# GpSimd takes the q and k products (from VectorE) and the residual adds (from DMA) in a fused linear-attention and gated-FFN kernel

## The chip, the cores and the metric

The kernel runs on one core of a Trainium2 chip. The metric is the device time of one execution in microseconds (us); less is better. Times are medians of several executions. A profiled execution gives the busy time of each engine, the waits and the exact order of the instructions. In the profile PE is TensorE's matmuls, PEld its weight loads, DVE is VectorE, ACT is ScalarE, POOL is GpSimd and SP is SyncE.

## The reference

A complex-decay linear attention feeds a gated feed-forward network, with the attention's result `x` added at the end.

```python
# q, k, v, a_re, a_im: (4, 8, 768, 48) float32
mag = sqrt(a_re**2 + a_im**2); scale = minimum(mag, 0.999) / (mag + 1e-6)
ar_n, ai_n = a_re * scale, a_im * scale
for t in range(768):                       # per batch and head, state 48 x 48
    S_re, S_im = ar*S_re - ai*S_im + k_t v_t^T,  ar*S_im + ai*S_re
    y_t = q_t @ S_re
x = y as (3072, 384)
g, val = x @ w_gate, x @ w_val             # 384 x 1536
res_gate = sigmoid(x @ w_res)              # 384 x 384
out = x + res_gate * ((gelu(g) * val) @ w_out)
```

The kernel does not walk the time steps. It takes 256 of them at once (a group `g`, two 128-row chunks). It builds the cumulated log decay and angle with matmuls against triangular matrices, takes `E = exp(+)`, `Ei = exp(-)` and the cosines and sines `CS`, and forms `Q = CS*(q*E)` and `K = CS*(k*Ei)`. Masked products of these give the attention within a group, and a small state is carried between groups.

## The kernel before

There are 12 groups in 7 units (1, 2, 2, 2, 2, 2 and 1 groups). The program alternates `phase_x(u)`, a *decay stretch*, and `phase_y(u)`, a *gate/value stretch*. In the decay stretch of unit `u` ScalarE makes the exponentials and sines of the next unit, and TensorE ends the attention of unit `u` and does the output matmuls of unit `u-1`. In the gate/value stretch TensorE runs the gate and value matmuls of unit `u`, while VectorE multiplies `q`, `k` by the decay for unit `u+1`. `weave` interleaves steps at issue; each engine then runs its own list strictly in order.

```python
ldv = pool("ldv", bufs=6); pK = pool("pK", bufs=1); xp = pool("xp", bufs=10); ob = pool("ob", bufs=2)
# (pool construction is shortened here)

def load_v(g):
    t = ldv.tile([128, C, H, D], BF, tag="v", name="v")
    for c in range(C):
        nc.gpsimd.dma_start(out=t[:, c], in_=rows(v, g, c))     # GpSimd's queue
    T["v", g] = t

def after_landing(t, f):                    # f's transfers start only once t has landed
    w = singles.tile([1, 1], FP, name="landed%d" % len(T))
    i = nc.gpsimd.tensor_copy(out=w, in_=t[0:1, C - 1, H - 1, D - 1:D])
    with tc.issue_after(i.ins):
        f()

def turn(nm, g, srcs):                      # decay rows, turned by way of DRAM
    md = dr.tile([n, DM], FP, tag="d" + nm, name="d" + nm)
    for i, src in enumerate(srcs):
        nc.gpsimd.dma_start(out=md[i:i + 1, :], in_=src)
    m = mp.tile([128, n, H], FP, tag=nm, name=nm)
    for u in range(2):
        nc.gpsimd.dma_start(out=m[u * D:(u + 1) * D].rearrange("p r h -> p (r h)"), in_=...)
    # ...

def products(g):
    def x0():
        qE = pK.tile([128, W], BF, tag="qE", name="qE")
        nc.vector.tensor_tensor(out=qE, in0=flat(T["q", g]), in1=T["E", g], op=OP.mult)
        T["qE", g] = qE
    def x1():
        kE = pK.tile([128, W], BF, tag="kE", name="kE")
        nc.vector.tensor_tensor(out=kE, in0=flat(T["k", g]), in1=T["Ei", g], op=OP.mult)
        T["kE", g] = kE
    def mk(nm, src):
        def x():                            # Q = CS*qE, K = CS*kE
            # ...
            nc.vector.tensor_tensor(out=t, in0=T["CS", g], in1=sb, op=OP.mult)
        return x
    return [x0, mk("Q", "qE"), x1, mk("K", "kE")]

def gv_step(u, ffi):
    # ... three matmuls into PSUM tile gp, three into vp
    act(out=h2[:, ffi, :], in_=gp, func=AF.Gelu)
    nc.vector.scalar_tensor_tensor(out=h2[:, ffi, :], in0=h2[:, ffi, :], scalar=0.5, in1=vp, ...)

def op_step(u, jj):
    # ... 12 matmuls into PSUM tile ps
    ot = ob.tile([128, DM], FP, tag="ot", name="ot")
    nc.vector.scalar_tensor_tensor(out=ot, in0=T["sg", u][:, jj], scalar=1.0, in1=ps, op0=OP.add, op1=OP.mult)
    t0 = token(u, jj) * 128
    if u == NU - 1:
        nc.vector.tensor_tensor(out=ot, in0=ot, in1=T["x", token(u, jj)], op=OP.add)
    nc.sync.dma_start(out=out[t0:t0 + 128, :], in_=ot)
    if u < NU - 1:                          # residual added by an accumulating DMA
        nc.gpsimd.dma_start(out=out[t0:t0 + 128, :], in_=T["x", token(u, jj)], accum_op=OP.add)

def phase_y(u):
    # ...
    pr = [st for g in gs(u + 1) for st in products(g)]
    weave((0.0, 1.0, gv), (0.0, 0.4, pr), (0.3, 0.95, att_steps(u + 1, 0)))

for u in range(-1, NU + 1):
    phase_x(u)
    # ... decay inputs of later units
    phase_y(u)
    for g in gs(u + 3):
        load_q(g)                           # q and k, on SyncE's queue
        after_landing(T["k", g], call(load_v, g))
```

## Time and profile before

| | before |
|---|---|
| time, median of 3 (range) | 324.13 us (323.16 to 324.32) |
| span of the profiled execution | 322.4 us |
| TensorE / VectorE / ScalarE / GpSimd busy | 84% / 73% / 65% / 25% |

The first part of the page gives each engine's busy time, share of the span and number of instructions.

```profile
PE 272.1 (84%) x2200; PEld 170.5 (53%) x2200; DVE 234.8 (73%) x431; ACT 209.8 (65%) x353; POOL 80.5 (25%) x115
```

A mean hides that the stretches have different limits, so the next view cuts the span. The table of windows has start and end, length, the busy time of each engine (instructions in brackets), the granted TensorE clock, the share of time that the 16 DMA engines were busy (summed so that it can pass 1) and the rate. I cut where ScalarE loads a new function table, which is where stretches begin. The rows are the gate/value stretch of unit 0, the decay stretch of unit 1 and the gate/value stretch of unit 1.

```profile
core 0: us, PE busy (x) PEld busy (x) DVE busy (x) ACT busy (x) POOL busy (x), PEclk, DMA share, GB/s
63.20:83.50 20.30, 19.24 (x224) 15.63 (x224) 16.25 (x36) 12.16 (x27) 3.87 (x6) 0.83 1.20 171
83.50:101.40 17.90, 14.09 (x81) 7.48 (x80) 13.59 (x24) 17.19 (x28) 3.93 (x6) 1.00 1.34 190
101.40:127.80 26.40, 25.30 (x269) 16.01 (x267) 23.53 (x42) 16.57 (x31) 8.37 (x12) 1.00 0.96 153
...
```

In gate/value stretches TensorE is nearly always busy (25.30 of 26.40 us); in decay stretches ScalarE is (17.19 of 17.90).

The groups of instructions (line, engine, operation, output and inputs, shapes, count, then busy us, mean ns, idle before it) give the price of the products on VectorE.

```profile
L309 DVE TENSOR_TENSOR qE<-q,E 128x768 bf16<-128x768 f32 x12 | 11.4, 950 | 6.8 <-DMA ar<-in_a_re_dram 3.5 <-ACT E L124 3.3
L321 DVE TENSOR_TENSOR Q<-CS,qE 128x1536 bf16<-128x1536 bf16 x12 | 11.4, 947 | 2.5 <-ACT CS L124 2.5
L314 DVE TENSOR_TENSOR kE<-k,Ei 128x768 bf16<-128x768 f32 x12 | 11.4, 946 | 0.0
```

The timeline of GpSimd between 50 and 86 us (start us, length us, instruction, and in brackets how long the engine waited and for what) shows the two small copies that hold back `v` until `k` has landed.

```profile
...
69.91 0.17 POOL L171 COPY landed<-k 1x1 f32<-1x1 f32 x1 [19.59 <-DMA k<-in_k_dram]
70.14 1.77 POOL L150 DMA_DIRECT2D v<-in_v_dram  x2
74.41 0.17 POOL L171 COPY landed<-k 1x1 f32<-1x1 f32 x1 [2.50 <-DMA k<-in_k_dram]
74.64 1.76 POOL L150 DMA_DIRECT2D v<-in_v_dram  x2
```

GpSimd has nothing else to do in that time, so a wait of 19.59 us costs nothing.

Finally the timeline of VectorE around the start of unit 1's gate/value stretch at 101.4 us.

```profile
100.11 0.94 DVE L321 TENSOR_TENSOR Q<-CS,qE 128x1536 bf16<-128x1536 bf16 x1
100.98 0.94 DVE L314 TENSOR_TENSOR kE<-k,Ei 128x768 bf16<-128x768 f32 x1
101.84 0.94 DVE L309 TENSOR_TENSOR qE<-q,E 128x768 bf16<-128x768 f32 x1
102.71 0.94 DVE L321 TENSOR_TENSOR K<-CS,kE 128x1536 bf16<-128x1536 bf16 x1
103.58 1.27 DVE L446 SCALAR_TENSOR_TENSOR h<-h,vp 128x512 bf16<-128x512 bf16 x2
```

The products run one after another at 0.94 us.

### The profile page before, as it was taken

The numbers are of one execution on the slowest core, as the hardware profiler recorded it, in microseconds if no ns is written. First come the engines' busy times: TensorE is split into PE (matmuls) and PEld (weight loads), VectorE is DVE, ScalarE is ACT, GpSimd is POOL, SyncE is SP. The second block draws the span as 40 slices with busy tenths as digits, with TensorE's granted clock in tenths as the row PEclk, the third lists the DMA queues.
The fourth block names the chain that finished last, engine by engine and source line by source line (L and its number), as shares of the span: only waits on it lengthen the run. The fifth ranks groups of instructions, "written<-read, shape, count | busy, mean of one in ns | idle before, by whom it ended". The sixth has DMA issues, their size and how long they took to land.

```text
span 322.4 us, 5853 instructions
## 1 busy us (share of the span) xinstructions
PE 272.1 (84%) x2200; PEld 170.5 (53%) x2200; DVE 234.8 (73%) x431; ACT 209.8 (65%) x353; POOL 80.5 (25%) x115
## 2 busy tenths in 40 slices
PE   0337927789887999789997999998999999899994
PEld 0116624677543666445664556554656655555682
DVE  2446769968499995599982999974899837864352
ACT  4549684646998557977568976569665683656150
POOL 1206522022040370259020572000630003200220
PEclk9995676959999999999999999999999999999998
DMA  8999999989999995396850595000360003600441
GB/s 159 218 183 181 182 169 165 185 174 180 187 179 186 223 160 33 76 197 113 122 36 2 107 121 95 2 0 3 75 122 3 2 0 76 122 2 0 107 91 50
DMA packets 137755, 34.55 MB, mean 107 GB/s; under 512 B 126848, under 2 KB 137728, under 8 KB 137728
## 3 DMA queue, kind: packets, MB, share of 16 engines
q1 hardware_dynamic: 103296, 23.60, 36.8%
q0 software_dynamic: 34432, 10.59, 31.2%
q8 instruction: 17, 0.28, 0.3%
q14 instruction: 10, 0.08, 0.1%
HBM read 31.31 MB, written 9.07 MB: 125 GB/s over the span
## 4 chain that ended last, share of the span: by engine, by line
PE 56%; SPq 12%; ACT 11%; DMA 9%; DVE 6%; issue 3%; POOL 1%; ACTq 0%; DVEq 0%; POOLq 0%
PE vp L443 14%; PE gp L439 13%; SPq L136 6%; SPq L144 6%; PE op L463 6%; DMA k<-in_k_dram 4%; PE rp L455 3%; PE tp L349 3%; PE tp L346 3%; PE at L356 3%; ACT L477 3%; DMA m<-dm 3%; ACT s L124 3%; PE cst L236 2%; PE y L394 2%
## 5 line engine op out<-in xcount | busy, mean ns | idle before, releaser
L124 ACT ACTIVATE h<-gp 128x512 bf16<-128x512 f32 (+1 forms) x84 | 44.5, 536 | 38.4 <-PE gp L439 37.9
L439 PE MATMUL gp<-xT,wg 128*128 128x512 bf16 (+1 forms) x252 | 65.4, 353 | 3.4 <-ACT h L124 2.0
L443 PE MATMUL vp<-xT,wv 128*128 128x512 bf16 (+1 forms) x252 | 66.6, 353 | 0.0
L446 DVE SCALAR_TENSOR_TENSOR h<-h,vp 128x512 bf16<-128x512 bf16 (+1 forms) x84 | 49.8, 603 | 16.4 <-PE vp L443 12.0
L463 PE MATMUL op<-wo,h 128*128 128x384 bf16 x288 | 50.2, 326 | 8.1 <-ACT Ei L124 5.9
L463 PEld LDWEIGHTS <-h 128*128 128x128 bf16 x288 | 27.8, 98 | 28.7 <-issue 11.3
L351 ACT COPY qk<-tp 96x512 bf16<-96x512 bf16 x48 | 27.9, 580 | 17.1 <-PE tp L349 7.9
L359 DVE TENSOR_TENSOR atm<-at,mask 128x512 bf16<-128x512 f32 x48 | 32.9, 686 | 8.2 <-PE at L356 7.8
L472 POOL DMA_DIRECT2D out_dram<-x x22 | 20.4, 947 | 54.4 <-DMA out_dram<-ot 43.1
L439 PEld LDWEIGHTS <-wg 128*128 128x128 bf16 x252 | 23.7, 99 | 17.9 <-issue 4.2
L443 PEld LDWEIGHTS <-wv 128*128 128x128 bf16 x252 | 23.8, 99 | 13.3
L189 DVE TENSOR_TENSOR ai<-s,ai 128x768 f32<-128x768 f32 x12 | 11.1, 955 | 23.6 <-ACT s L124 23.6
L477 ACT ACT_TABLE_LOAD x21 | 26.9, 1283 | 1.1 <-PEq L615 0.7
L346 PE MATMUL tp<-ident,Q 128*96 128x128 bf16 x192 | 20.1, 231 | 6.9 <-DVE Q L321 6.2
L346 PEld LDWEIGHTS <-Q 128*96 128x96 bf16 x192 | 17.4, 130 | 15.3 <-DVE Q L321 10.0
L124 ACT ACTIVATE CS<-fg,hpi 128x768 bf16<-128x768 f32 x12 | 11.2, 935 | 20.8 <-DVE fg L246 20.7
L150 POOL DMA_DIRECT2D v<-in_v_dram x24 | 21.9, 932 | 4.2 <-DMA v<-in_v_dram 1.3
L349 PE MATMUL tp<-ident,K 128*96 128x128 bf16 x192 | 22.3, 235 | 0.0
L236 PE MATMUL cst<-ai,lt0b 128*128 128x384 f32 x24 | 11.8, 577 | 11.7 <-ACT ai L124 11.0
L352 DVE COPY qk<-tp 96x512 bf16<-96x512 bf16 x48 | 19.8, 413 | 2.3 <-ACT qk L351 1.7
L212 PE MATMUL csl<-ar,lt0a 128*128 128x384 f32 x24 | 11.4, 562 | 10.8 <-DMA ar<-in_a_re_dram 10.8
L466 DVE SCALAR_TENSOR_TENSOR ot<-sg,op 128x384 f32<-128x384 f32 x24 | 13.1, 547 | 10.1 <-PE op L463 10.1
(85 smaller groups left out, 522.0 us busy)
## 6 DMA issues: line engine op xcount, KB each, us to landing
ar<-in_a_re_dram SPq DMA_DIRECT2D x24, 192.0 KB, 4.7
ai<-in_a_im_dram SPq DMA_DIRECT2D x24, 192.0 KB, 4.1
q<-in_q_dram SPq DMA_DIRECT2D x24, 192.0 KB, 3.8
k<-in_k_dram SPq DMA_DIRECT2D x24, 192.0 KB, 3.7
out_dram<-ot SPq DMA_DIRECT2D x24, 192.0 KB, 2.5
out_dram<-x POOLq DMA_DIRECT2D x22, 192.0 KB, 3.7
v<-in_v_dram POOLq DMA_DIRECT2D x24, 96.0 KB, 5.0
wg<-in_moe_w_gate_dram POOLq DMA_DIRECT2D x4, 288.0 KB, 11.4
```

The lines of the kernel that those rows point to most:

```text
L124: tab(nc.scalar.activation(**kw))
L150: nc.gpsimd.dma_start(out=t[:, c], in_=rows(v, g, c))
L346: nc.tensor.transpose(out=tp[0:DD, j * 128:j * 128 + 128], in_=Q(x), identity=ident)
L349: nc.tensor.transpose(out=tp[0:DD, 512 + j * 128:640 + j * 128], in_=K(x), identity=ident)
L351: nc.scalar.copy(out=qk[0:DD, 0:512], in_=tp[0:DD, 0:512])
L359: nc.vector.tensor_tensor(out=atm, in0=at, in1=mask4, op=OP.mult)
L439: nc.tensor.matmul(out=gp, lhsT=wg[:, fi, ffi * 128:(ffi + 1) * 128], rhs=xT[:, fi, :], start=(fi == 0), stop=(fi == KD - 1))
L443: nc.tensor.matmul(out=vp, lhsT=wv[:, fi, ffi * 128:(ffi + 1) * 128], rhs=xT[:, fi, :], start=(fi == 0), stop=(fi == KD - 1))
L446: nc.vector.scalar_tensor_tensor(out=h2[:, ffi, :], in0=h2[:, ffi, :], scalar=0.5, in1=vp, op0=OP.mult, op1=OP.mult)
L463: nc.tensor.matmul(out=ps, lhsT=h2[:, ffi, jj * 128:(jj + 1) * 128], rhs=wo[:, ffi, :], start=(ffi == 0), stop=(ffi == KF - 1))
L472: nc.gpsimd.dma_start(out=out[t0:t0 + 128, :], in_=T["x", token(u, jj)], accum_op=OP.add)
L477: tab(nc.scalar.preload_act_table_set(nm))
```

## The change

VectorE looks loaded (73%) and GpSimd free (25%). The change gives GpSimd the 24 products `q*E` and `k*Ei`, those of `q` only after the sines, with a second buffer each (`v` and `x` lose one of theirs). GpSimd also adds `x` into the output tile, so that one store is enough and the 22 accumulating DMAs go. The decay rows move to SyncE's queue, to leave GpSimd free. `v` loads lose the wait for `k` in later units and are issued ahead of the gate/value stretch; only the loads issued at `u = -1` keep it. The four steps of a group are issued as qE, kE, Q, K.

```diff
-    ldv = ctx.enter_context(tc.tile_pool(name="ldv", bufs=6))
+    ldv = ctx.enter_context(tc.tile_pool(name="ldv", bufs=5))
-    pK = ctx.enter_context(tc.tile_pool(name="pK", bufs=1))
+    pK = ctx.enter_context(tc.tile_pool(name="pK", bufs=2))
-    xp = ctx.enter_context(tc.tile_pool(name="xp", bufs=10))
+    xp = ctx.enter_context(tc.tile_pool(name="xp", bufs=9))
@@ p2_sin
+        T["sin"] = T["tab"]
@@ turn: both DMA issues
-            nc.gpsimd.dma_start(...)
+            nc.sync.dma_start(...)
@@ products
-            nc.vector.tensor_tensor(out=qE, in0=flat(T["q", g]), in1=T["E", g], op=OP.mult)
+            i = nc.gpsimd.tensor_tensor(out=qE, in0=flat(T["q", g]), in1=T["E", g], op=OP.mult)
+            tc.add_manual_dep(i.ins, T["sin"].ins.name, behind, reason="after the sines")
-            nc.vector.tensor_tensor(out=kE, in0=flat(T["k", g]), in1=T["Ei", g], op=OP.mult)
+            nc.gpsimd.tensor_tensor(out=kE, in0=flat(T["k", g]), in1=T["Ei", g], op=OP.mult)
@@ op_step
-        if u == NU - 1:
-            nc.vector.tensor_tensor(out=ot, in0=ot, in1=T["x", token(u, jj)], op=OP.add)
+        eng = nc.vector if u == NU - 1 else nc.gpsimd
+        eng.tensor_tensor(out=ot, in0=ot, in1=T["x", token(u, jj)], op=OP.add)
         nc.sync.dma_start(out=out[t0:t0 + 128, :], in_=ot)
-        if u < NU - 1:
-            nc.gpsimd.dma_start(out=out[t0:t0 + 128, :], in_=T["x", token(u, jj)], accum_op=OP.add)
@@ phase_y
-        pr = [st for g in gs(u + 1) for st in products(g)]
+        pr = [pp[i] for pp in [products(g) for g in gs(u + 1)] for i in (0, 2, 1, 3)]
@@ main loop
+        if u > 0:
+            for g in gs(u + 2):
+                load_v(g)
         phase_y(u)
         for g in gs(u + 3):
             load_q(g)
-            after_landing(T["k", g], call(load_v, g))
+            if u < 0:
+                after_landing(T["k", g], call(load_v, g))
```

More of the change, by code (lines that the diff above doesn't have):

```diff
@@ L115 @@
     order = mybir.DependencyInfo(mybir.DependencyClass.NoSync, mybir.DependencyReason.DATA)
+    behind = mybir.DependencyInfo(mybir.DependencyClass.Sync, mybir.DependencyReason.DATA)
     def tab(ins):
@@ L261, in turn @@
         for i, src in enumerate(srcs):
-            nc.gpsimd.dma_start(out=md[i:i + 1, :], in_=src)
+            nc.sync.dma_start(out=md[i:i + 1, :], in_=src)
         m = mp.tile([128, n, H], FP, tag=nm, name=nm)
         for u in range(2):
-            nc.gpsimd.dma_start(out=m[u * D:(u + 1) * D].rearrange("p r h -> p (r h)"),
+            nc.sync.dma_start(out=m[u * D:(u + 1) * D].rearrange("p r h -> p (r h)"),
                                 in_=md.rearrange("r (h d) -> d (r h)", h=H))
```

## The prediction

> **What bounds it now.** The table of windows gives three regimes. (a) 0–58 us: loads and a serial ScalarE/VectorE chain; TensorE is busy 29 of 58 us. (b) Later, long gate/value stretches with TensorE saturated (25.9 of 26.0, 26.4 of 26.4, 26.3 of 26.3 us). (c) Between them, 14–20 us decay stretches in which ScalarE leads (17.1 of 19.2 us) and TensorE idles 1–4 us each, about 12 us in all. VectorE is 73% busy, but only in (c) does it hold anything: the timeline shows the sines waiting 1.16 + 0.83 us (and 0.93 + 1.16) for the fractions.
>
> **What the change does.**
> - 24 products leave VectorE (groups: 0.95 us each, 22.8 us; about 2 precede the sines of each decay stretch). No GpSimd product is in this trace. The Trainium skill, "GPSIMD Engine Reference", section "Performance versus the Vector engine", has a two-input add 1.96 times slower there; my estimate from it is 1.8 us a product, 43 us in all, plus 22 residual adds of about 1 us.
> - 22 accumulating DMAs (0.95 us of GpSimd each, 3.7 us to land) go; the DMA queues are nearly idle by then (share 0.1–0.3), so this is off the path. The adds lengthen the two-buffer output chain by about 1 us, mostly hidden.
> - Decay rows leave GpSimd; in the chain of waits they cost perhaps 3 us. SyncE can block behind stores, so I credit 1–2 us.
>
> **Gain.** At most the idle TensorE time of (c) less what comes from other causes (about 1.5 us per stretch is the wait for ScalarE's exponentials to free PSUM). I expect 1 us a stretch, and 1 us at the start: 4–6 us. "SBUF — State Buffer", section "Who interferes with whom", says a GpSimd op and a VectorE op with two SBUF inputs block each other; K's product on VectorE now starts together with q's on GpSimd: under 1 us, hidden.
>
> **Loss, which I expect to decide.** GpSimd runs in order. In its new order the q products of unit 1 stand *behind* the two "landed" copies that gate v on k of groups 3 and 4, and behind six v issues. In the trace those copies run at 69.9 and 74.4 us (GpSimd timeline), because loads are rate-bound then (DMA share 1.2–1.3, 175 GB/s), which the change doesn't alter. An issue costs 0.88 us. So the q product starts not at about 61 us, when the sines end, but at about 78; Q is ready near 81, against 60.5 now. VectorE and TensorE run in order too: Q's product stands before the h products, so after about 3 of 12 gate/value steps both stop near 65 us. What TensorE did from 65.5 to 82.8 us comes after 81: first decay matmul of the next stretch near 97–98 instead of 82.8. Loss about 15 us. Later loads don't suffer: the next q load was issued only at 82.8 us anyway. Later stretches have no such gate.
>
> 324 + 15 − 5, rounded down: **333 us, 8 in 10 between 320 and 342**. Chances: faster by over 2% 0.08, within 2% 0.27, slower by over 2% 0.65.
>
> **What would show it.** Right: GpSimd waits for k until about 74 us, first unit-1 q product near 78, TensorE idle 12–17 us within 62–82, its idle in later decay stretches down to 1–3 us; products 1.6–2.0 us; VectorE busy near 212 us. Wrong: q products at 60–65 us; then 317–321 us.
>
> **What would make it wrong.** Loads landing much earlier; steps that fill the pause; GpSimd products of 3 us or more, which would stall every gate/value stretch; SyncE blocked by decay rows so that loads or stores come late.

## The result

| | before | after |
|---|---|---|
| time, median of 4 (range), us | 324.23 (323.16 to 324.34) | 362.86 (362.28 to 363.81) |
| ratio | | 1.121 (95%: 1.1175 to 1.1246) |
| span of the profiled execution, us | 322.4 | 360.2 |

All outputs are right. A ratio here is always the mean time of one kernel's fast runs over that of the other's of the same rounds, so it is not quite the ratio of the medians quoted. Executions over 1.5% slower than the fastest of the same kernel are left out of the means. Each batch of experiments has its own runs of the kernel before on the same chip; the medians of their fast executions lay between 323.4 and 324.3 us.

The change costs 38.6 us. I had predicted 333 us, with 320 to 342.

First, busy time by engine after the change.

```profile
PE 281.4 (78%) x2200; PEld 172.9 (48%) x2200; DVE 235.3 (65%) x407; ACT 210.4 (58%) x353; POOL 108.7 (30%) x97
```

VectorE has 24 instructions fewer (431 to 407), which had cost 22.8 us, and yet is as busy as before: 235.3 us against 234.8. The remaining instructions have become 235.3 - (234.8 - 22.8) = 23.3 us longer. The groups show it on two of them, and show the new GpSimd work.

```profile
L318 POOL TENSOR_TENSOR kE<-k,Ei 128x768 bf16<-128x768 f32 x12 | 26.0, 2173 | 84.1 <-ACT Ei L126 81.6
L473 POOL TENSOR_TENSOR ot<-ot,x 128x384 f32<-128x384 f32 x22 | 23.2, 1057 | 58.8 <-DVE ot L470 32.2
...
L312 POOL TENSOR_TENSOR qE<-q,E 128x768 bf16<-128x768 f32 x12 | 25.7, 2160 | 6.5 <-ACT CS L126 6.5
...
L325 DVE TENSOR_TENSOR Q<-CS,qE 128x1536 bf16<-128x1536 bf16 x12 | 15.3, 1272 | 16.0 <-POOL qE L312 15.9
```

The `Q` product, which nobody touched, went from 947 to 1272 ns on average. A mean that rises by a third can be all of them a little or a few of them a lot; the view by source line, with shortest, median and longest ns, says which. The first line is the kernel before.

```profile
L321 DVE TENSOR_TENSOR Q<-CS,qE x12: 940/946/958, 23.3 to 274.7; 128x1536 bf16<-128x1536 bf16 x12
```

```profile
L325 DVE TENSOR_TENSOR K<-CS,kE x12: 942/958/2595, 24.2 to 309.2; 128x1536 bf16<-128x1536 bf16 x12
L325 DVE TENSOR_TENSOR Q<-CS,qE x12: 942/946/2552, 26.7 to 311.8; 128x1536 bf16<-128x1536 bf16 x12
```

Most take what they took before, and some take up to 2.6 us. The extra 1.6 us is nearly a whole GpSimd product (1.8 us when undisturbed). That looks like waiting, not like slower arithmetic. `atm`, an operation of VectorE with an input in PSUM, stays at 677 to 693 ns throughout.

The table of windows, for the stretches shown of before:

```profile
core 0: us, PE busy (x) PEld busy (x) DVE busy (x) ACT busy (x) POOL busy (x), PEclk, DMA share, GB/s
65.80:100.40 34.60, 18.05 (x212) 14.62 (x213) 16.78 (x33) 12.29 (x28) 11.08 (x12) 0.70 1.40 177
100.40:119.90 19.50, 15.49 (x93) 8.12 (x92) 15.74 (x24) 17.67 (x28) 7.66 (x6) 1.00 0.90 138
119.90:150.90 31.00, 27.89 (x266) 16.95 (x267) 24.30 (x39) 16.72 (x32) 7.52 (x6) 0.89 0.40 55
...
```

The first stretch grew from 20.3 to 34.6 us, with TensorE no busier (18.05 us). The third grew from 26.4 to 31.0 us; there TensorE got 27.89 us busy at a granted clock of 0.89 instead of 1.00, and VectorE 24.30 us busy although two of the products that left it (0.94 us each) had run in this stretch.

The first stretch is the stall that I had predicted. The timeline of GpSimd:

```profile
...
51.90 7.18 POOL L318 TENSOR_TENSOR kE<-k,Ei 128x768 bf16<-128x768 f32 x2
72.00 0.17 POOL L173 COPY landed<-k 1x1 f32<-1x1 f32 x1 [12.92 <-DMA k<-in_k_dram]
72.24 1.82 POOL L152 DMA_DIRECT2D v<-in_v_dram  x2
76.00 0.17 POOL L173 COPY landed<-k 1x1 f32<-1x1 f32 x1 [1.95 <-DMA k<-in_k_dram]
76.24 3.51 POOL L152 DMA_DIRECT2D v<-in_v_dram  x4
79.74 3.60 POOL L312 TENSOR_TENSOR qE<-q,E 128x768 bf16<-128x768 f32 x2
```

And TensorE, which stopped at 69.4 us:

```profile
84.22 0.66 PE L350 MATMUL tp<-ident,Q 128*96 128x128 bf16 x4 [14.86 <-DVE Q L325]
```

The second kind of loss is seen at the start of unit 1's gate/value stretch (119.9 us), in VectorE's timeline.

```profile
118.12 1.67 DVE L325 TENSOR_TENSOR K<-CS,kE 128x1536 bf16<-128x1536 bf16 x1
119.71 0.55 DVE L226 TENSOR_TENSOR P<-ai 128x384 f32<-128x384 f32 x1
120.29 2.04 DVE L228 TENSOR_TENSOR P<-P 128x384 f32<-128x384 f32 x1
122.26 0.54 DVE L409 CAST Gb<-dk 96x384 bf16<-96x384 f32 x1
122.73 2.08 DVE L325 TENSOR_TENSOR K<-CS,kE 128x1536 bf16<-128x1536 bf16 x1
124.73 0.54 DVE L374 TENSOR_TENSOR G<-dk,M 96x384 f32<-96x384 f32 x1
125.20 0.67 DVE L450 SCALAR_TENSOR_TENSOR h<-h,vp 128x512 bf16<-128x512 bf16 x1
```

Two adds of the same shape stand one after the other, 0.55 and 2.04 us. In the same microseconds GpSimd runs two `q` products, from 120.03 to 123.99. The first `h` product comes 5.3 us into the stretch instead of 2.2. No bracket marks an idle time: to the profile VectorE is *busy* while it waits.

Cutting every profiled execution at ScalarE's table loads gives a ledger. Y is a gate/value stretch, X a decay stretch. The rows below the first two are experiments that the next section tells of.

| stretch, us | start | Y0 | X1 | Y1 | X2 | Y2 | X3 | Y3 | X4 | Y4 | X5 | rest |
|---|---|---|---|---|---|---|---|---|---|---|---|---|
| before | 63.2 | 20.3 | 17.9 | 26.4 | 19.2 | 26.0 | 19.6 | 26.4 | 17.4 | 26.3 | 12.0 | 47.7 |
| after | 65.8 | 34.5 | 19.5 | 31.0 | 20.5 | 29.6 | 20.2 | 27.4 | 17.4 | 28.8 | 14.5 | 51.0 |
| e1, `v` ungated | 66.9 | 21.4 | 19.5 | 31.2 | 20.5 | 29.6 | 20.2 | 27.4 | 17.4 | 28.8 | 14.4 | 51.2 |
| e3, q on VectorE | 68.9 | 19.5 | 19.2 | 26.0 | 20.4 | 27.2 | 21.8 | 26.6 | 19.5 | 27.2 | 13.1 | 48.7 |
| e2, both on VectorE | 65.2 | 19.0 | 17.9 | 25.6 | 19.7 | 25.8 | 19.1 | 26.8 | 17.0 | 26.4 | 12.6 | 48.7 |
| e9, adds undone too | 65.2 | 19.0 | 17.6 | 25.6 | 19.5 | 25.7 | 19.1 | 26.4 | 16.6 | 26.1 | 11.9 | 47.5 |

After minus before: 14.2 us in Y0, 15.0 in Y1 to Y4 and the rest, 6.0 in the decay stretches, 2.6 at the start; together 37.8, the difference of the two spans.

### The profile page after: what moved, and what is told of

It is laid out like the page before. It is cut to its first block, busy times and chain, and to the rows that moved or that the text cites. A ratio compares the mean times of both kernels' runs of the same rounds, so it can differ in the third digit from the quotient of the medians.

```text
span 360.2 us, 5879 instructions
## 1 busy us (share of the span) xinstructions
PE 281.4 (78%) x2200; PEld 172.9 (48%) x2200; DVE 235.3 (65%) x407; ACT 210.4 (58%) x353; POOL 108.7 (30%) x97
## 3 DMA queue, kind: packets, MB, share of 16 engines
q0 software_dynamic: 30144, 6.20, 19.2%
## 4 chain that ended last, share of the span: by engine, by line
PE 47%; SPq 20%; issue 11%; DVE 8%; ACT 6%; POOL 6%; DMA 2%; POOLq 0%; DVEq 0%; ACTq 0%
PE vp L447 11%; PE gp L443 10%; SPq L138 10%; SPq L146 9%; PE op L467 6%; PE rp L459 3%; POOL qE L312 3%; PE tp L350 3%; PE tp L353 3%; PE at L360 3%; DVE Q L325 2%; PE y L398 2%; POOL ot L473 2%; ACT s L126 2%; DVE K L325 2%
## 5 line engine op out<-in xcount | busy, mean ns | idle before, releaser
L443 PE MATMUL gp<-xT,wg 128*128 128x512 bf16 (+1 forms) x252 | 68.3, 363 | 4.4 <-DVE xT L434 4.4
L447 PE MATMUL vp<-xT,wv 128*128 128x512 bf16 (+1 forms) x252 | 67.9, 363 | 0.0
L450 DVE SCALAR_TENSOR_TENSOR h<-h,vp 128x512 bf16<-128x512 bf16 (+1 forms) x84 | 50.6, 605 | 19.0 <-PE vp L447 14.1
L467 PE MATMUL op<-wo,h 128*128 128x384 bf16 x288 | 51.8, 333 | 7.8 <-ACT Ei L126 4.9
L318 POOL TENSOR_TENSOR kE<-k,Ei 128x768 bf16<-128x768 f32 x12 | 26.0, 2173 | 84.1 <-ACT Ei L126 81.6
L363 DVE TENSOR_TENSOR atm<-at,mask 128x512 bf16<-128x512 f32 x48 | 33.1, 690 | 16.6 <-PE at L360 16.4
L473 POOL TENSOR_TENSOR ot<-ot,x 128x384 f32<-128x384 f32 x22 | 23.2, 1057 | 58.8 <-DVE ot L470 32.2
L152 POOL DMA_DIRECT2D v<-in_v_dram x24 | 21.5, 903 | 63.2 <-PE y L400 37.7
L447 PEld LDWEIGHTS <-wv 128*128 128x128 bf16 x252 | 24.7, 101 | 15.7 <-issue 1.9
L312 POOL TENSOR_TENSOR qE<-q,E 128x768 bf16<-128x768 f32 x12 | 25.7, 2160 | 6.5 <-ACT CS L126 6.5
L191 DVE TENSOR_TENSOR ai<-s,ai 128x768 f32<-128x768 f32 x12 | 11.1, 955 | 24.0 <-ACT s L126 17.7
L325 DVE TENSOR_TENSOR Q<-CS,qE 128x1536 bf16<-128x1536 bf16 x12 | 15.3, 1272 | 16.0 <-POOL qE L312 15.9
L390 PE MATMUL dk<-v,K 128*96 128x48 bf16 x160 | 12.3, 217 | 16.8 <-DVE K L325 11.6
L470 DVE SCALAR_TENSOR_TENSOR ot<-sg,op 128x384 f32<-128x384 f32 x24 | 13.2, 548 | 15.4 <-PE op L467 12.7
## 6 DMA issues: line engine op xcount, KB each, us to landing
wv<-in_moe_w_val_dram POOLq DMA_DIRECT2D x4, 288.0 KB, 11.9
```

The costliest lines, as they stand in the source:

```text
L312: i = nc.gpsimd.tensor_tensor(out=qE, in0=flat(T["q", g]), in1=T["E", g], op=OP.mult)
L363: nc.vector.tensor_tensor(out=atm, in0=at, in1=mask4, op=OP.mult)
L443: nc.tensor.matmul(out=gp, lhsT=wg[:, fi, ffi * 128:(ffi + 1) * 128], rhs=xT[:, fi, :], start=(fi == 0), stop=(fi == KD - 1))
L447: nc.tensor.matmul(out=vp, lhsT=wv[:, fi, ffi * 128:(ffi + 1) * 128], rhs=xT[:, fi, :], start=(fi == 0), stop=(fi == KD - 1))
L467: nc.tensor.matmul(out=ps, lhsT=h2[:, ffi, jj * 128:(jj + 1) * 128], rhs=wo[:, ffi, :], start=(ffi == 0), stop=(ffi == KF - 1))
L473: eng.tensor_tensor(out=ot, in0=ot, in1=T["x", token(u, jj)], op=OP.add)
```

## The experiments

The theory at this point had two parts. (1) The stall of Y0 comes from the `q` products standing behind the `v` gate on GpSimd. (2) All the rest comes from GpSimd's operations that read SBUF, because VectorE and GpSimd then block each other. The Trainium skill, "SBUF — State Buffer", section "Who interferes with whom", says that they share a port pair, held by one of them at a time, so that a VectorE instruction with two SBUF inputs blocks against a GpSimd instruction that reads SBUF, and not against one that only writes. The main rivals to (2) were that VectorE merely waits for GpSimd's results (latency), that the moved adds hold up the two-buffer output chain, and that the DMA queues got in the way.

Unless said otherwise, an experiment starts from the changed kernel.

### Run e1: the v gate taken out of GpSimd's order

```diff
-        if u > 0:
+        if u >= 0:
             for g in gs(u + 2):
                 load_v(g)
@@
             load_q(g)
-            if u < 0:
-                after_landing(T["k", g], call(load_v, g))
```

> The changed kernel, but v of groups 3 and 4 is issued without waiting for k to land, so the q products of unit 1 no longer stand behind that gate on GpSimd. Queue theory (the stall at 66 to 84 us is only the place in GpSimd's order): first unit-1 q product at 62 to 70 us instead of 79.7, the first gate/value stretch shrinks from 34.6 to 20 to 24 us, total 349 to 353 us against 363. Rival (the loads themselves hold the stretch, whatever the order): that stretch stays over 30 us and the total over 359.

Measured: 349.41 us (347.83 to 352.7), ratio 1.0802 (1.0724 to 1.0881). Against after that is 362.9 - 349.4 = 13.5 us less. The timeline of GpSimd shows the copies gone and the `q` product 12.7 us earlier.

```profile
...
60.34 3.58 POOL L318 TENSOR_TENSOR kE<-k,Ei 128x768 bf16<-128x768 f32 x2
63.86 1.84 POOL L152 DMA_DIRECT2D v<-in_v_dram  x2
67.00 5.61 POOL L312 TENSOR_TENSOR qE<-q,E 128x768 bf16<-128x768 f32 x2 [1.31 <-ACT CS L126]
...
```

In the ledger Y0 falls from 34.5 to 21.4 us, and apart from a slower start (1.1 us) no other stretch moves by more than 0.2 us. Part (1) is shown, and its worth is 13.5 us. 25 us are left.

### Runs e2 and e3: the products back on VectorE

e3 puts back only `q`'s product, e2 both. The rest of the change stays.

```diff
-            i = nc.gpsimd.tensor_tensor(out=qE, in0=flat(T["q", g]), in1=T["E", g], op=OP.mult)
-            tc.add_manual_dep(i.ins, T["sin"].ins.name, behind, reason="after the sines")
+            nc.vector.tensor_tensor(out=qE, in0=flat(T["q", g]), in1=T["E", g], op=OP.mult)
@@ e2 only
-            nc.gpsimd.tensor_tensor(out=kE, in0=flat(T["k", g]), in1=T["Ei", g], op=OP.mult)
+            nc.vector.tensor_tensor(out=kE, in0=flat(T["k", g]), in1=T["Ei", g], op=OP.mult)
```

> The changed kernel with both products back on VectorE; residual adds on GpSimd, decay rows on SyncE and the new v loads stay. If the products on GpSimd cause the whole loss: 321 to 326 us, as before. If residual adds or decay rows share in it (adds holding the output buffers, SyncE blocked behind stores): 330 us or more, with the decay stretches still 20 us and more.

> The changed kernel with only q's product back on VectorE; k's stays on GpSimd. If the loss lies in q's product being late and sharing the port with K and Q at the start of each gate/value stretch: 324 to 330 us, gate/value stretches back to about 26.4 us, the decay stretches keep what k's product costs there (VectorE's tensor_scalar of the decay logs at 1.3 us instead of 0.55). If the k product matters as much: 340 us or more.

Measured: e2 327.21 us (325.94 to 329.51; a fourth execution, of 330.88 us, is left out), ratio 1.0121 (1.0065 to 1.0176). With that one the median is 328.36 us; this is the 328.4 us of the later expectations, which were written with it. e3 339.60 us (337.14 to 341.01), ratio 1.0485 (1.0434 to 1.0536).

So 35.7 of the 38.6 us hang on the products, and `k`'s share is not small: 339.6 - 327.2 = 12.4 us. e2 fell between the two forecasts that I had for it. My expectation for e3 was a miss. I had taken `k`'s product for harmless, because nobody waits long for it; but it runs early, among the two-input operations of the decay stretch, and the ledger shows e3 against e2 losing 1.3, 0.7, 2.7 and 2.5 us in X1 to X4, and 3.7 us at the start, where one add of VectorE takes 4.56 us beside two `k` products. (The profiled execution of e2 is its fastest, so the ledger shows such differences a little large.) The rival about the DMA queues can hold no more than what e2 has left.

### Run e5: q's product not held until after the sines

```diff
-            i = nc.gpsimd.tensor_tensor(out=qE, ...)
-            tc.add_manual_dep(i.ins, T["sin"].ins.name, behind, reason="after the sines")
+            nc.gpsimd.tensor_tensor(out=qE, ...)
```

> The changed kernel without the dependence of q's product on the sines, so both products run on GpSimd as soon as the exponentials are there, ahead of the v gate. If lateness is what costs: first stretch about 20 us, later ones about 26.5 us, total 325 to 333 us. If contention for the shared port costs most, wherever the products run: the same VectorE time is lost in the decay stretches, which grow to 21 us and more, total 338 us or more.

Measured: 352.61 us (350.1 to 354.14; a fourth execution, of 356.49 us, is left out), ratio 1.0885 (1.0823 to 1.0947). The early product stands ahead of the `v` gate, and Y0 is 20.2 us, as before. But the decay stretches grow: X1 to X4 are 22.0, 21.7, 24.2 and 21.3 us, against 19.5, 20.5, 20.2 and 17.4 of after. Its timelines show GpSimd's products beside VectorE's work. These are lines of GpSimd's timeline,

```profile
98.06 2.13 POOL L312 TENSOR_TENSOR qE<-q,E 128x768 bf16<-128x768 f32 x1
...
100.14 2.13 POOL L317 TENSOR_TENSOR kE<-k,Ei 128x768 bf16<-128x768 f32 x1
```

and these of VectorE's.

```profile
98.43 2.17 DVE L200 TENSOR_SCALAR ar<-ar 128x768 f32<-128x768 f32 x1
100.53 2.56 DVE L199 SCALAR_TENSOR_TENSOR ar<-s,ar 128x768 f32<-128x768 f32 x1
```

Undisturbed these take 0.55 and 0.95 us. Note that L200 has a single input: it is a `tensor_scalar`, one of the operations that the skill's section names as able to use both port pairs. The dependency ("only once the sines are done") was a good one for the decay stretches, and a bad one for Y0.

### Runs e6 and e7: GpSimd work that nobody reads

These two separate occupancy from latency. Both start from e2, where VectorE makes its own products, and add GpSimd work with a result that is thrown away. e6 reads SBUF (the same `q` product again), e7 only writes it (three memsets, of 0.74 us each).

```diff
@@ e6, in x0 after VectorE's product
+            z = pK.tile([128, W], BF, tag="z", bufs=1, name="z")
+            i = nc.gpsimd.tensor_tensor(out=z, in0=flat(T["q", g]), in1=T["E", g], op=OP.mult)
+            tc.add_manual_dep(i.ins, T["sin"].ins.name, behind, reason="after the sines")
@@ e7, in the same place
+            for _ in range(3):
+                z = pK.tile([128, W], BF, tag="z", bufs=1, name="z")
+                i = nc.gpsimd.memset(z, 0.0)
+                tc.add_manual_dep(i.ins, T["sin"].ins.name, behind, reason="after the sines")
```

> The kernel with both products on VectorE (328 us, profile 323.8) plus a GpSimd product of q and E after the sines whose result nobody reads: nothing waits for it, it only occupies GpSimd and what it shares with VectorE. Port theory: the VectorE operations with two SBUF inputs that start beside it (K, Q, P) take 1.5 to 2.6 us at worst instead of 0.95 or 0.55, each full gate/value stretch grows by 1 to 2.5 us, total 333 to 340 us. Lateness theory (only the dependence of Q on GpSimd's result costs): no change, 325 to 330 us.

> The same with three GpSimd memsets of 128x768 in the place of the unread product: about as much GpSimd time [...], but no SBUF reads. Port theory in the form of the skill's page (VectorE operations with two inputs share only the read side): K, Q and P keep 0.95 and 0.55 us, total as without them, 325 to 330 us. If any busy GpSimd slows VectorE: as the unread product, 333 us or more.

Measured: e6 338.30 us (336.97 to 339.41), ratio 1.0446 (1.0407 to 1.0484). e7 329.45 us (327.35 to 330.88), ratio 1.0175 (1.0117 to 1.0233). Against e2's 327.2 us, the product that nobody reads costs 11.1 us, and memsets of at least as much GpSimd time (3 x 0.74 us for each 1.8 us product) cost about 2 (e2 ran on another chip; its range overlaps that of e7, whose verdict is unclear). The view by tile of e6 (shortest, median, longest ns):

```profile
L327 DVE TENSOR_TENSOR K<-CS,kE x12: 943/950/2574, 24.8 to 286.6; 128x1536 bf16<-128x1536 bf16 x12
```

```profile
L314 POOL TENSOR_TENSOR z<-q,E x12: 1802/1812/2578, 24.0 to 285.8; 128x768 bf16<-128x768 f32 x12
```

And of e7:

```profile
L328 DVE TENSOR_TENSOR K<-CS,kE x12: 943/948/951, 24.5 to 278.8; 128x1536 bf16<-128x1536 bf16 x12
```

```profile
L315 POOL MEMSET z<- x36: 731/738/830, 23.7 to 279.6; 128x768 bf16 x36
```

`K`'s longest is 2574 ns beside GpSimd reads and 951 ns beside GpSimd writes. Nobody waits for `z`, so this is blocking and not latency. The view of `z` in e6 lists no waiter at all, so nothing waited for the buffers that it reads either; and e7 keeps GpSimd as long from its adds as e6 does (26.8 us of memsets against 23.9 of products). VectorE's busy time tells the same: 246.3 us in e6 against 236.3 in e2, with the same 431 instructions.

### Run e13: the same for k's product

```diff
@@ from e2, in x1 after VectorE's product
+            z = pK.tile([128, W], BF, tag="z", bufs=1, name="z")
+            nc.gpsimd.tensor_tensor(out=z, in0=flat(T["k", g]), in1=T["Ei", g], op=OP.mult)
```

> Both products on VectorE, residual adds on GpSimd (328.4 us), plus an unread GpSimd product of k and its exponential as soon as that is there, beside VectorE's own. If k's product on GpSimd cost 11 us by occupying the port (VectorE's operations on the decay logs at up to 2.2 us): 335 to 342 us, most of it in the decay stretches. If it cost by being late for K: 327 to 331 us.

Measured: 345.39 us (343.46 to 347.15), ratio 1.0636 (1.0542 to 1.073), which is 18.2 us over e2 and above the 335 to 342 us of my forecast. X2, X3 and X4 take 23.2, 21.8 and 20.2 us (19.7, 19.1 and 17.0 in e2). The view by source line (in e2 the longest is 959 ns):

```profile
L199 DVE SCALAR_TENSOR_TENSOR ar<-s,ar x12: 943/950/2565, 9.8 to 241.9; 128x768 f32<-128x768 f32 x12
```

So 12 unread `k` products cost 18 us, and in e3, where they also relieve VectorE of 11.4 us of its own work, the cost is still 12.4. The relief is not worth the blocking.

### Runs e9, e10, e14, e12: what the residual adds cost

e2 is still 1.2% slower than before. e9 takes e2 and brings back the accumulating DMA; e10 keeps the GpSimd add but gives the output tile three buffers instead of two, and e14 is e10 again, because the profiled execution of e10 came out at 1534.39 us (I don't know why, and it is not used).

```diff
@@ e9, in op_step
-        eng = nc.vector if u == NU - 1 else nc.gpsimd
-        eng.tensor_tensor(out=ot, in0=ot, in1=T["x", token(u, jj)], op=OP.add)
+        if u == NU - 1:
+            nc.vector.tensor_tensor(out=ot, in0=ot, in1=T["x", token(u, jj)], op=OP.add)
         nc.sync.dma_start(out=out[t0:t0 + 128, :], in_=ot)
+        if u < NU - 1:
+            nc.gpsimd.dma_start(out=out[t0:t0 + 128, :], in_=T["x", token(u, jj)], accum_op=OP.add)
@@ e10 and e14
-    ob = ctx.enter_context(tc.tile_pool(name="ob", bufs=2))
+    ob = ctx.enter_context(tc.tile_pool(name="ob", bufs=3))
```

> Both products on VectorE and the residual added by the accumulating DMA again; decay rows stay on SyncE. If the GpSimd adds cost by contention or by holding the two output buffers: 2 to 4 us faster than 328.4 us, 324 to 326 us. If the accumulating DMAs were a burden, as the change supposes: 329 to 332 us.

> Both products on VectorE, residual adds on GpSimd, decay rows on SyncE (328.4 us), with three output buffers for two. If the adds cost because they hold an output buffer longer: 323 to 326 us. If they cost because they wait for, and block, the port shared with VectorE: no change, 327 to 330 us.

> The run with three output buffers again, because its profile fell into one execution of 1534 us. Buffers theory: VectorE's waits before the gated output fall, total 323 to 326 us. Otherwise 327 to 331 us as its timed runs.

Measured: e9 323.16 us (322.23 to 324.12), ratio 0.998 (0.9949 to 1.0011), so the adds cost 327.2 - 323.2 = 4.0 us. In e9 no `q` or `k` product of VectorE is lengthened; in e2 some `k` products take 1.18 to 1.49 us beside an add. e10 327.39 us (median of the four fast executions of six), ratio 1.0116 (1.0082 to 1.0149); e14 328.31 us (two executions), ratio 1.0111 (0.9988 to 1.0235, unclear). A third buffer changes nothing, so the buffer rival falls.

e12 takes e9 and adds an unread GpSimd add of the same size, which waits for the same instruction as the real one did.

```diff
-        nc.vector.scalar_tensor_tensor(out=ot, ...)
+        j = nc.vector.scalar_tensor_tensor(out=ot, ...)
@@
+            z = pK.tile([128, DM], FP, tag="z", bufs=1, name="z")
+            i = nc.gpsimd.tensor_tensor(out=z, in0=T["sg", u][:, jj], in1=T["x", token(u, jj)], op=OP.add)
+            tc.add_manual_dep(i.ins, j.ins.name, behind, reason="with the residual")
             nc.gpsimd.dma_start(out=out[t0:t0 + 128, :], in_=T["x", token(u, jj)], accum_op=OP.add)
```

> The kernel with accumulating DMAs (323.2 us) plus, beside each of the 22, a GpSimd add of gate and x of the same shape whose result nobody reads. If the residual adds cost 5 us because GpSimd is busy on the shared port in the decay stretches: 326 to 329 us. If they cost because the store now waits for the add: no change, 322 to 325 us.

Measured: 326.38 us (325.51 to 328.33), ratio 1.0036 (0.9947 to 1.0125). This is inconclusive as a time: the fast executions of the kernel before themselves spread from 323.2 to 328.0 us. By stretches of its profile, Y3, X4, Y4 and X5 are 26.8, 17.0, 26.4 and 12.5 us, as in e2 (26.8, 17.0, 26.4, 12.6) and not as in e9 (26.4, 16.6, 26.1, 11.9), so there the add costs by running at all. The last stretch is 47.6 us, as in e9, against 48.7 in e2: about 1.1 us there goes with the store waiting for the add. From the first gate/value stretch on, e12 takes 257.9 us, e9 254.9 and e2 258.6, so most of the cost goes with the add running at all; the rest of e12's longer profile lies before, where VectorE waits 3.34 us for `k`'s transfer (1.61 in e9). These are single executions: how the 4 us split stays open.

### Runs e8 and e11: the decay rows

e8 takes e2 and puts the decay rows back on GpSimd's queue. e11 takes the kernel *before* and moves only the decay rows to SyncE's queue.

```diff
@@ turn, both issues; e8 from e2 (e11 the other way round, from before)
-            nc.sync.dma_start(...)
+            nc.gpsimd.dma_start(...)
```

> Both products on VectorE and the decay rows back on GpSimd's queue; residual adds stay on GpSimd. If the decay rows on SyncE are a gain as the change intends: 1 to 3 us slower than the 328.4 us with them on SyncE. If they block SyncE's stores and loads: 1 to 4 us faster, 324 to 327 us.

> The kernel before with the decay rows on SyncE's queue and nothing else changed. If that part alone is a gain: 320 to 323 us, the gain in the decay stretches after unit 2, where the chain of waits of before holds the decay rows. If not: 323 to 326 us, because stores and loads on SyncE stand behind waits for the decay rows.

Measured: e8 332.52 us (331.0 to 334.38), ratio 1.0271 (1.0226 to 1.0317): beside GpSimd's adds the move saves 332.5 - 327.2 = 5.3 us, more than the 1 to 3 that I expected. e11 321.99 us (321.05 to 322.48, 6 executions), ratio 0.995 (0.993 to 0.997): alone it saves 1.5 us. This is the only part of the change that gains, and e11 is the only version whose interval lies below the kernel before, by half a per cent.

### Runs b2 and b3: attempts at a faster kernel

Both start from e9. b3 puts back the old order of the four steps; b2 uses the old order only for `u <= 0`, which was to unite the best stretches of both.

```diff
-        pr = [pp[i] for pp in [products(g) for g in gs(u + 1)] for i in (0, 2, 1, 3)]
+        pr = [pp[i] for pp in [products(g) for g in gs(u + 1)] for i in ((0, 1, 2, 3) if u <= 0 else (0, 2, 1, 3))]
@@ b3: the condition is always true
```

> A version meant to win: both products on VectorE, residual by the accumulating DMA, decay rows on SyncE, two buffers per product, v loads as in the change, and the new order of products only after unit 1 (before: 63.2 us to the first gate/value stretch, the new order: 65.2). If the new order in unit 1 costs those 2 us: 320.5 to 322 us. Otherwise as e9, 323 us.

> The same with the old order of products everywhere. If the new order gains nothing later: within 0.5 us of b2_mixed. If it does gain 0.2 to 0.8 us a stretch, as the e9 profile suggests: 1 to 3 us slower than b2_mixed.

Measured: b2 324.47 us (321.5 to 325.77; three of the six executions, of 327.01 to 327.57 us, are left out), ratio 1.001 (0.9959 to 1.0061); b3 323.54 us (322.52 to 327.05), ratio 1.0012 (0.9973 to 1.0051). Neither wins. The order of steps, the extra buffers and the early `v` loads are worth nothing that these runs can show. Why b2 spreads so far is not settled. In its profiled execution, a slow one, the first gate/value stretch begins at 69.9 us instead of the 65.2 of e9, and VectorE waits 5.00 us there for `k`'s transfer (1.61 in e9): its later landing is 3.4 of the 5.4 us between these two profiles.

### The sum

Taken out one after another, in this order, the parts of the change are worth, in medians:

| step | us | worth of the part |
|---|---|---|
| after | 362.9 | |
| e1: `v` gate no longer ahead of q's products | 349.4 | 13.5 |
| e3: q's products on VectorE (gate back, harmless now) | 339.6 | 9.8 |
| e2: k's products on VectorE | 327.2 | 12.4 |
| e9: residual by accumulating DMA | 323.2 | 4.0 |
| before: decay rows, `v` loads, order, buffers | 323.7 | -0.5 |

The parts interact (the decay rows are worth 5.3 us beside the adds and 1.5 alone), so another order would give somewhat other terms.

## Why the prediction was wrong

**The bound (right, but incomplete).** TensorE does lead the gate/value stretches and ScalarE the decay stretches. But I wrote that VectorE, 73% busy, holds anything only in the decay stretches. It was busy 23.53 of 26.40 us in Y1, in order, and it empties TensorE's PSUM tiles. After the change its first `h` product there came 3.1 us later (5.3 us into the stretch against 2.2), which is more than the 2.9 us that it had to give.

**The stall in Y0 (right).** Predicted: first `q` product near 78 us, `Q` ready near 81, TensorE idle 12 to 17 us, loss about 15. Measured: `q` product at 79.74, idle 14.86 in one piece, loss 14.2 in the ledger and 13.5 by e1. `Q` was ready at 84.2, 3 us later than I said: its own product took 2.55 us because it started (81.61) beside the second `q` product. I had written the blocking down and did not see it at work in the very instruction that I was timing.

**Price of a GpSimd product (right alone, low in use).** The Trainium skill, "GPSIMD Engine Reference", section "Performance versus the Vector engine", gives a two-input add as 1.96 times slower than on VectorE, from which I estimated 1.8 us. The shortest here is 1797 ns against VectorE's 950, a factor of 1.9, so the trace agrees. In use the mean is 2160 to 2173 ns, because GpSimd is blocked too; two `k` products at 51.90 us took 7.18.

**The step that failed: the blocking.** My text: "K's product on VectorE now starts together with q's on GpSimd: under 1 us, hidden." I knew the rule, applied it to one pair of instructions, and took its size from nothing. In its place the runs show:
- The unread `q` products cost the kernel 11.1 us (e6), the unread `k` products 18.2 (e13), memsets of the same length about 2 (e7). In the change itself the products stand for 9.8 us (q, beyond the gate) and 12.4 us (k), both net of the VectorE work that they save.
- The blocking meets VectorE operations with two SBUF inputs, and `tensor_scalar` and casts too: a `tensor_scalar` of 0.55 us took up to 2.17 (e5), a cast of 0.34 us took 1.95 (e6, at 108.66 us). The sum over VectorE is 23.3 us, so that my mark "VectorE busy near 212 us" failed as well (235.3).

**The gain (wrong sign).** "I expect 1 us a stretch" in the decay stretches; they lost 6.0 us in all. TensorE's idle time in X1 to X5 (length less busy time) was to fall; it rose from 11.7 to 16.1 us. Over the whole kernel neither the move of the products nor that of the adds gained. The work that left VectorE came back as waiting on VectorE.

**The residual adds (wrong).** "About 1 us, mostly hidden"; they cost 4.0 us (e9). It is not the two-buffer chain that I named (e10, e14).

**The decay rows (right).** Credited with 1 to 2 us; 1.5 alone (e11).

The sum that I should have made is 324 + 14 (gate) + 10 + 12 + 4 (q's products, k's products, adds) - 1, about 363. I had the gate and left out the next two, and had put the adds at 1 and a gain of 5 in their place.

How much of the `q` product's 9.8 us is `Q` waiting for its input? The trace of after narrows it: VectorE sat idle for `qE` 15.9 us in all, 14.17 of them in Y0, and the rest here.

```profile
228.42 0.96 DVE L325 TENSOR_TENSOR Q<-CS,qE 128x1536 bf16<-128x1536 bf16 x1 [0.51 <-POOL qE L312]
...
311.84 1.65 DVE L325 TENSOR_TENSOR Q<-CS,qE 128x1536 bf16<-128x1536 bf16 x1 [1.24 <-POOL qE L312]
```

In e1, where the gate is gone, it is 2.8 us in three places. In Y1, which lost most after Y0, VectorE never waits for `qE` in either run. e6 costs about as much without any such wait, though in other stretches: against e2, Y1 grows by 1.6 us, Y4 by 5.4 and the last stretch by 3.4 (in e1 against e3, Y1 grows by 5.2). Which operations collide depends on the timing, so that the two totals are alike is partly luck. The granted clock was lower too in Y1 of after (0.89 against 1.00); no run separates its part, which stays open.

## What to carry to other kernels

In these runs an idle GpSimd was not free capacity for operations that read SBUF: count what it adds to the engine that it shares ports with, over every VectorE instruction that runs beside it, before counting what it takes off. Before moving work, put a copy of it with an unread result on the other engine; one run gives the price without the benefit. And when an engine runs in order, look for what waits ahead of the moved instruction: a gate that was free while the engine was idle becomes a stall once something urgent stands behind it.

## What the Trainium skill lacked or had wrong

- "SBUF — State Buffer", section "Who interferes with whom": the rule held in the two runs that test it, reads (e6, `K` up to 2574 ns) against writes (e7, up to 951 ns). It does not say how blocking looks in a profile: it is not idle time with a releaser but a longer instruction. VectorE stayed 235 us busy with 22.8 us of work removed. The sign to look for is a longest time far over the median for one shape (942/946/2552 ns).
- "Perfetto Trace Analysis", section "Identifying the Most-Contended Engine", calls occupancy a fair measure of how close VectorE and GpSimd are to roofline. Here it was not: some 23 of VectorE's 235.3 us after the change were waiting, counted as busy.
- "SBUF — State Buffer", the same section "Who interferes with whom", speaks of the pair being held for one whole instruction. Some operations waited through several: in e6 a GpSimd add of 0.91 us took 4.16 us (from 102.58 us) while VectorE ran four two-input operations back to back until 105.98, and in e3 an add of 0.55 us on VectorE took 4.56 (52.23 to 56.79) while GpSimd ran two products (52.77 to 56.37). In other places one got through between two (`P<-P` above). The page does not say when the other side gets its turn.
- "GPSIMD Engine Reference", section "Performance versus the Vector engine": 1.96 is the ratio of the operation alone (here 1797 over 950 ns, 1.9). What a moved operation costs a kernel with a busy VectorE is not on the page: 12 unread products of 1.8 us, 22 us of GpSimd time, cost 11.1 us of kernel time in one place and 18.2 in another.
